# Block-diagonal attention and a gated FFN on one core: first loads in two-token runs, weight signs by a leaky slope, separate first buffers

## The chip, the cores and the metric

The kernel runs on one core of a Trainium2 chip. The core has five engines that work side by side: PE (TensorE, matmuls and the loading of their weights), DVE (VectorE), ACT (ScalarE), POOL (GpSimd), and SP (SyncE), which here issues all DMAs on one queue that 16 DMA engines serve. The metric is the device time of one execution in microseconds (us); the median of 3 runs before is 494.02 us.

## The reference

Attention inside chunks of 64 tokens, for 8 batches, 8 heads, 576 tokens and head size 64, and then an FFN with a gate made by a convolution over 3 neighbouring tokens:

```python
scores = scale * np.matmul(q_c, k_c.transpose(0, 1, 2, 4, 3))     # chunks of 64 tokens
attn = np.exp(scores - np.max(scores, axis=-1, keepdims=True))
attn = attn / (np.sum(attn, axis=-1, keepdims=True) + 1e-09)
x = np.matmul(attn, v_c)                       # then to [8, 576, 512]
h = np.maximum(x @ w_in, 0.0)                  # 512 -> 1024
conv_out[s] = sum(conv_w[k] * h[s + k - 1] for k in range(3))     # zeros beyond the ends
out = (h * sigmoid(conv_out)) @ w_out          # 1024 -> 512
```

q, k and v arrive as float32. [...]

## The kernel before, in words

**Tiles.** 4608 tokens make 36 tiles of 128 (two chunks of 64, not always of one batch). The FFN works on 16 units of 288 tokens: the first matmul of the FFN (`mm1`, L334) runs over a unit with 2 neighbours, in 8 blocks f of 128 hidden columns; the second (`mm2`, L388) over tiles of 128 tokens. Both are made of three products of high and low parts (`x_h`, `x_l`, `wi_h`, `wi_l` and so on), to reach f32 precision with rounded inputs. An `mm1` block is 12 matmuls, an `mm2` step 3.

**A tile of attention.** `load_rows` (L113) loads q and k of tiles 0 to 8 by rows, tokens in partitions, so that a run in memory is one token of one head, 64 numbers. Later tiles come through `load_group` in another layout and are transposed by DVE. `load_v` loads v in four DMAs of 64 partitions. For tiles 0 to 8 `t_pe` (L164) transposes q and then k on PE, four matmuls each into a PSUM bank; `t_copy` (L168, ACT) copies them out. Then come `scores` (L200: 16 matmuls of 64x64), maximum and subtraction (L210, L214, DVE), exp (L223, ACT), sum and reciprocal (L230 to L236, DVE), division (L262, POOL), transpose of the probabilities (`p_pe`, L269, PE), copy (L274, ACT), attention times v (`attn_v`, L283, PE), and the split into `x_h` (L319, ACT) and `x_l` (L323, DVE). The first unit of the FFN needs tiles 0 to 2.

**Weights.** `split` turns a piece of weights into high and low parts. `w_load` (L408) brings it into one of two places (`w_slots`) as low and high words L and H. `w_scale` (L421, ACT) scales H, read as an f32; `w_shift` (L425, DVE) shifts the exponent into place, which throws the sign out; `w_words` (L430, DVE) puts in the upper bits of L; `w_sgn` (L435, DVE) puts back the sign from H, after which the place is free; `w_hi` (L471, ACT) rounds to the high part, and `w_left` (L439, POOL) subtracts for the low part. This happens ten times in 8 MB of weights; conv_w takes another path.

**Places.** Two places for rows (`slots`) and two for weights (`w_slots`) are cut out of the same two tiles of the pool `raw` (L106 to L108), which later hold the groups of q and k.

**The order.** All work is entered as steps with an engine, a cost, and what each needs and frees. A list of step numbers, `order_`, gives the order of all steps, and so of the instructions on each engine and of SP's DMAs. Costs and lags of the steps give each a begin and an end. Where that plan leaves PE idle in the first 110 us, it puts transposes of the identity (L907), one for each 0.14 us, into a free bank; nobody reads their result:

```python
            for _ in range(int((begin[i] - pe_free) / 0.14) if idle else 0):
                nc.tensor.transpose(out=banks[idle[-1]][:, 0:P], in_=ident, identity=ident)
```

They are instructions like others: once built in, they run, whether PE has something to wait for or not.

Of the kernel before, what the change touches and what calls it, by code (L numbers as in the profile page):

```python
# [30 lines left out]
def attn_ffn(ctx: ExitStack, tc: tile.TileContext, q, k, v, w_in, conv_w, w_out, out):  # L31
    nc = tc.nc
# [24 lines left out]
    TP = 12  # L57
    scale = 1.0 / float(D) ** 0.5

    const = ctx.enter_context(tc.tile_pool(name="const", bufs=1))  # L60
    raw = ctx.enter_context(tc.tile_pool(name="raw", bufs=2))
# [5 lines left out]
    work7 = ctx.enter_context(tc.tile_pool(name="work7", bufs=7))  # L67
    ps_s = ctx.enter_context(tc.tile_pool(name="ps_s", bufs=1, space=PSUM))
# [37 lines left out]
    spare = [raw.tile([P, 2 * G * 4 * TG * 32], F32, name="qk") for _ in range(2)]  # L106
    slots = [sp[:, 2048:3072] for sp in spare]
    w_slots = [sp[:, 0:2048] for sp in spare]  # L108
# [14 lines left out]
    def load_group(j):  # L123

        groups[j] = r = raw.tile([P, 2, G, 4 * TG, 32], F32, name="qk")
# [17 lines left out]
    def load_v(st, t):  # L143
# [8 lines left out]
        for s in range(2):  # L152
            b, t0 = chunk(2 * t + s)
            for hp in range(2):
                j0 = 64 * (hp ^ s)
                nc.sync.dma_start(out=r[j0:j0 + C, :, s, :], in_=v[b, hp::2, t0:t0 + C, :].rearrange("g j d -> j g d"))  # L156


    def t_pe(st, i):

        tp = banks[st["tp", i]]
        rows = row_slot(st)[:, 512 * i:512 * i + 512]
        for g in range(G):
            nc.tensor.transpose(out=tp[:, P * g:P * g + P], in_=rows[:, P * g:P * g + P], identity=ident)  # L164

    def t_copy(st, i):
        st[i] = tT = work.tile([P, G, 2 * C], F32, name="qk"[i] + "T")
        nc.scalar.copy(out=tT, in_=banks[st["tp", i]].rearrange("p (g i) -> p g i", i=P))  # L168
# [107 lines left out]
    def attn_v(st):  # L276
        for g in range(G):
            for s in range(2):
                for hp in range(2):
                    j0, n, m = C * (hp ^ s), s, s  # L280
# [137 lines left out]
    def w_scale(st):  # L418

        st["T"] = w_tile(st, "wt")  # L420
        nc.scalar.mul(out=st["T"], in_=st["H"].bitcast(F32), mul=2.0 ** -112)  # L421
# [10 lines left out]

    def w_sgn(st):
        T = st["T"].bitcast(U32)
        nc.vector.scalar_tensor_tensor(out=T, in0=st["H"], scalar=0x80000000, in1=T,  # L435
                                       op0=ALU.bitwise_and, op1=ALU.bitwise_or)
# [62 lines left out]
    def split(key, t_load, src, hi=None, lo=None, lo_pool=False, half=False):  # L499
# [19 lines left out]
        s3 = step("DVE", b, key + 0.01, w_words, (st,), [s2], port=True)  # L519
        s4 = step("DVE", b, key + 0.02, w_sgn, (st,), [s3], free=["wslot"], port=True)  # L520
# [8 lines left out]
    def att(t, key, load_key, writes):  # L529

        st = {"t": t}
        if t < NAT:
            r = "wslot" if t in W_ROWS else "slot"
            ld = step("SP", 1.2 if (2 * t) % NCK < NCK - 1 else 2.3, load_key, load_rows, (st, t), take=[(r, st)], lag=3.3)
            tt = []
            for i in range(2):
                s = step("PE", 0.44, key - 3, t_pe, (st, i), [ld, before.get("t")], take=[("bk", st, ("tp", i)), "qk"[i] + "T"], free=[r] if i else [])
                before["t"] = s
                tt.append(step("ACT", 0.59, key - 3, t_copy, (st, i), [s], free=[("bk", ("tp", i))]))
# [7 lines left out]
        ldv = step("SP", 2.2 if t < TP else 0.5 if (2 * t) % NCK < NCK - 1 else 1.0, load_key + 0.05 if t < 5 else key - 8, load_v, (st, t), [before.get("v")], take=["v"], lag=1.66)  # L547
# [137 lines left out]
    for u in range(NU + 1):  # L685
# [267 lines left out]
```

## Time and profile before

| | before |
|---|---|
| median of 3 runs | 494.02 us (493.81 to 494.75) |
| profiled execution | 494.31 us, span 492.4 us |
| PE, DVE, ACT, POOL busy | 485.1, 350.4, 298.8, 191.6 us |
| granted TensorE clock | 1.000 |
| DMA | 50.16 MB in 185905 packets, of which 175068 under 512 B |
| filler L907 on PE | 160 transposes |
| first `mm1` matmul (L334) starts | 35.91 us |

The span runs from the first to the last instruction of the profiled execution; some 1.9 us of its time lie around it. Busy time on PE counts the filler too. A wait on a row of the profile is idle time of an engine, put down to what ended last before it went on.

### The profile page before, as it was taken

What the parts mean: (1) busy time and instruction counts of PE and PEld (TensorE: products, weight loads), DVE (VectorE), ACT (ScalarE), POOL (GpSimd) and SP (SyncE); (2) the same over time, 40 slices, a digit from 0 to 9 for tenths busy, and PEclk for the clock granted to TensorE, in tenths of its full rate; (3) what the DMA queues carried; (4) which work ended last, traced back from release to release, by engine and by line L of the source; (5) the groups of instructions that cost most, each with busy time, mean ns of one, the idle gap of its engine ahead of it and who ended that gap; (6) DMA issues with size and microseconds to landing.
All of it is one profiled execution on the core that took longest, in us unless ns stands there. A gap on an engine that the chain in (4) does not pass through costs nothing.

```text
span 492.4 us, 12912 instructions
## 1 busy us (share of the span) xinstructions
PE 485.1 (99%) x4985; PEld 436.2 (89%) x4985; DVE 350.4 (71%) x736; ACT 298.8 (61%) x749; POOL 191.6 (39%) x261
## 2 busy tenths in 40 slices
PE   8999999999999999999999999999999999999997
PEld 8889989999888998989888999899988988999885
DVE  3889998687566778886857887888878685574300
ACT  4479988875634675765635767566665564775501
POOL 1253538433314161534543173415253515244300
PEclk9999999999999999999999999999999999999999
DMA  8998964423255664436555553236561111100102
GB/s 196 232 233 240 236 166 79 71 46 57 64 124 114 134 156 73 96 68 137 89 116 133 119 87 75 62 70 137 103 166 46 44 44 44 47 19 2 43 23 85
DMA packets 185905, 50.16 MB, mean 102 GB/s; under 512 B 175068, under 2 KB 178164, under 8 KB 185844
## 3 DMA queue, kind: packets, MB, share of 16 engines
q1 hardware_dynamic: 185844, 49.34, 44.6%
q8 instruction: 39, 0.64, 0.6%
q14 instruction: 22, 0.18, 0.1%
HBM read 36.72 MB, written 9.44 MB: 94 GB/s over the span
## 4 chain that ended last, share of the span: by engine, by line
PE 93%; DMA 2%; DVE 2%; ACT 1%; SPq 1%; issue 0%; ACTq 0%
PE b_ps L388 41%; PE b_ps L334 41%; PE sx_ps L200 3%; PE sx_ps L283 2%; DMA qk<-in_moe_w_in 2%; PE z_ps L283 1%; PE b_ps L164 1%; PE z_ps L200 1%; PE b_ps L269 1%; PE b_ps L907 1%; DVE wt L430 1%; SPq L156 0%; DVE wt L435 0%; ACT wt L421 0%; ACT wi_h L471 0%
## 5 line engine op out<-in xcount | busy, mean ns | idle before, releaser
L379 POOL TENSOR_TENSOR g_l<-c,g_h 128x288 fp32r<-128x288 f32 (+8 forms) x184 | 109.9, 620 | 162.2 <-ACT g_h L375 132.0
L388 PE MATMUL b_ps<-wo_h,g_h 128*128 128x512 f32 x288 | 115.6, 401 | 0.0
L388 PE MATMUL b_ps<-wo_h,g_l 128*128 128x512 f32 x288 | 113.6, 395 | 0.0
L388 PE MATMUL b_ps<-wo_l,g_h 128*128 128x512 f32 x288 | 113.4, 394 | 0.0
L350 DVE SCALAR_TENSOR_TENSOR c<-b_ps,cw,c 128x287 f32<-128x287 f32 (+1 forms) x128 | 65.2, 512 | 46.0 <-ACT c L346 45.8
L334 PE MATMUL b_ps<-x_h,wi_h 128*128 128x290 f32 x512 | 90.6, 299 | 0.0
L334 PE MATMUL b_ps<-x_l,wi_h 128*128 128x290 f32 x512 | 89.5, 297 | 0.0
L334 PE MATMUL b_ps<-x_h,wi_l 128*128 128x290 f32 x512 | 89.1, 296 | 0.0
L334 PEld LDWEIGHTS b_ps<-x_h,wi_h 128*128 128x128 f32 x512 | 79.3, 189 | 7.5 <-DVE c L365 0.2
L341 ACT ACTIVATE b_ps<-b_ps 128x290 f32<-128x290 f32 x128 | 50.9, 399 | 53.3 <-PE b_ps L334 52.6
L362 ACT ACTIVATE c<-c 128x288 f32<-128x288 f32 x128 | 56.4, 443 | 43.6 <-DVE c L356 43.1
L365 DVE SCALAR_TENSOR_TENSOR c<-c,b_ps 128x288 f32<-128x288 f32 x128 | 56.7, 447 | 28.6 <-ACT c L362 27.9
L334 PEld LDWEIGHTS b_ps<-x_l,wi_h 128*128 128x128 f32 x512 | 75.9, 190 | 0.0
L334 PEld LDWEIGHTS b_ps<-x_h,wi_l 128*128 128x128 f32 x512 | 75.4, 189 | 0.0
L346 ACT ACTIVATE c<-b_ps,cw 128x288 f32<-128x288 f32 x128 | 63.4, 500 | 7.0
L356 DVE SCALAR_TENSOR_TENSOR c<-b_ps,cw,c 128x288 f32<-128x288 f32 (+1 forms) x128 | 64.9, 511 | 2.8
L388 PEld LDWEIGHTS b_ps<-wo_h,g_l 128*128 128x128 f32 x288 | 54.2, 188 | 12.6
L375 ACT CAST g_h<-c 128x288 fp32r<-128x288 f32 (+8 forms) x184 | 58.7, 357 | 9.2 <-DVE c L365 7.2
L388 PEld LDWEIGHTS b_ps<-wo_h,g_h 128*128 128x128 f32 x288 | 54.4, 189 | 9.3
L388 PEld LDWEIGHTS b_ps<-wo_l,g_h 128*128 128x128 f32 x288 | 54.3, 188 | 8.3
L245 POOL TENSOR_TENSOR wt<-wt,z 128x512 f32<-128x512 f32 x24 | 25.1, 1051 | 63.5 <-DVE z L233 14.3
L393 ACT ACTIVATE wt<-b_ps 128x512 f32<-128x512 f32 x36 | 21.4, 598 | 35.7 <-PE b_ps L388 27.4
(64 smaller groups left out, 495.1 us busy)
## 6 DMA issues: line engine op xcount, KB each, us to landing
out<-wt SPq DMA_DIRECT2D x36, 256.0 KB, 2.4
v<-in_v SPq DMA_DIRECT2D x21, 256.0 KB, 3.4
qk<-in_q SPq DMA_DIRECT2D x96, 48.0 KB, 2.3
qk<-in_k SPq DMA_DIRECT2D x96, 48.0 KB, 2.3
qk<-in_moe_w_out SPq DMA_DIRECT2D x4, 1024.0 KB, 6.5
v<-in_v SPq DMA_DIRECT2D x48, 64.0 KB, 3.6
wt<-wt SPq DMA_DIRECT2D x48, 64.0 KB, 2.1
qk<-in_q SPq DMA_DIRECT2D x96, 24.0 KB, 1.9
```

Of the source, the lines that this page charges most:

```text
L245: nc.gpsimd.tensor_tensor(out=two(st, "to"), in0=two(st, "of"), in1=z, op=ALU.mult)
L334: nc.tensor.matmul(h_ps[:, 0:hi - lo], lhsT=wt[:, f // 2, kt, P * (f % 2):P * (f % 2) + P], rhs=xt[:, u % NX, kt, 0:hi - lo], start=n == 0 ...
L341: nc.scalar.activation(out=h, in_=h, func=AF.Relu)
L346: nc.scalar.mul(out=st["c"], in_=banks[st["h"]][:, i0:i0 + st["n"]], mul=cw[:, FT + f:FT + f + 1])
L350: nc.vector.scalar_tensor_tensor(out=c[:, a:n], in0=banks[st["h"]][:, i0 + a - 1:i0 + n - 1], scalar=cw[:, f:f + 1], in1=c[:, a:n], op0=AL ...
L356: nc.vector.scalar_tensor_tensor(out=c[:, 0:b], in0=banks[st["h"]][:, i0 + 1:i0 + 1 + b], scalar=cw[:, 2 * FT + f:2 * FT + f + 1], in1=c[: ...
L362: nc.scalar.activation(out=st["c"], in_=st["c"], func=AF.Tanh, scale=0.5)
L365: nc.vector.scalar_tensor_tensor(out=st["c"], in0=st["c"], scalar=1.0, in1=banks[st["h"]][:, st["i0"]:st["i0"] + st["n"]], op0=ALU.add, op ...
L375: nc.scalar.copy(out=g_h[:, f, gs], in_=st["c"][:, cs])
L379: nc.gpsimd.tensor_tensor(out=g_l[:, f, gs], in0=st["c"][:, cs], in1=g_h[:, f, gs].bitcast(F32), op=ALU.subtract)
L388: nc.tensor.matmul(banks[st["o"]], lhsT=gt[:, f, o:o + P], rhs=wt[:, f, :], start=f == 0 and n == 0, stop=f == FT - 1 and n == 2)
L393: nc.scalar.mul(out=st["os"], in_=banks[st["o"]], mul=0.5)
```

## The change

- q and k of tiles 0 to 4 (`NP = 5`): a partition takes two neighbouring tokens instead of one, so that a run in memory is 128 numbers. q goes into the even partitions, k into the odd ones. `t_pe` picks them out with every other column of the identity (`ident[:, i::2]`), in 16 matmuls that contract over 128 partitions and have 64 columns on each side, in place of 4 transposes; `t_copy` puts even and odd tokens back in turn.
- The sign of the weights: `w_scale` is an activation with a leaky slope. A negative number is multiplied by another 2^32, which sets the bit that the shift moves into the sign's place. `w_sgn` goes, and `w_words` frees the place.
- Places for rows and weights are four tiles of a pool of their own, closed when the first group is loaded.
- v of tiles 0 to 11 in 3 DMAs where both chunks are of one batch (4 before, and 4 still where they aren't); which of the two chunks a half of `v` holds changes with it.
- The costs in the plan follow (`t_pe` 0.9 for 0.44, lags of the loads), and `order_` is another list: the order of most steps is new.

```diff
+    NP = 5
...
-    spare = [raw.tile([P, 2 * G * 4 * TG * 32], F32, name="qk") for _ in range(2)]
-    slots = [sp[:, 2048:3072] for sp in spare]
-    w_slots = [sp[:, 0:2048] for sp in spare]
+    places = sb_w.enter_context(tc.tile_pool(name="first", bufs=1))
+    slots = [places.tile([P, 2 * DM], F32, name=f"qk{i}") for i in range(2)]
+    w_slots = [places.tile([P, 4 * DM], F32, name=f"w{i}") for i in range(2)]
...
     def load_rows(st, t):
+        if t < NP:
+            r = row_slot(st).rearrange("(p two) (h c) -> two p h c", two=2, h=H)
...
+                    nc.sync.dma_start(out=r[i, p0:p0 + n], in_=src[b, :, t_:t_ + 2 * n, :].rearrange("h (p e) d -> p h (e d)", e=2))
...
     def load_group(j):
-        groups[j] = r = raw.tile([P, 2, G, 4 * TG, 32], F32, name="qk")
+        if not groups:
+            sb_w.close()
+            groups["raw"] = ctx.enter_context(tc.tile_pool(name="raw", bufs=2))
+        groups[j] = groups["raw"].tile([P, 2, G, 4 * TG, 32], F32, name="qk")
...
-        for s in range(2):
-            b, t0 = chunk(2 * t + s)
-            for hp in range(2):
-                j0 = 64 * (hp ^ s)
-                nc.sync.dma_start(out=r[j0:j0 + C, :, s, :], in_=v[b, hp::2, t0:t0 + C, :].rearrange("g j d -> j g d"))
+        (b0, t0), (b1, t1) = chunk(2 * t), chunk(2 * t + 1)
+        for hp in range(2):
+            for b, t_, j0, n in [(b0, t0, 0, P)] if b0 == b1 and not hp else [(b0, t0, C * hp, C), (b1, t1, C - C * hp, C)]:
+                nc.sync.dma_start(out=r[j0:j0 + n, :, hp, :], in_=v[b, hp::2, t_:t_ + n, :].rearrange("g j d -> j g d"))
...
+        if st["t"] < NP:
+            r = row_slot(st).rearrange("p (g u e d) -> p g u e d", g=G, u=2, e=2)
+            for g in range(G):
+                for e in range(2):
+                    for u in range(2):
+                        nc.tensor.matmul(tp.rearrange("p (g e n) -> p g e n", g=G, e=2)[D * u:D * u + D, g, e],
+                                         lhsT=r[:, g, u, e], rhs=ident[:, i::2], start=True, stop=True)
+            return
...
-        nc.scalar.mul(out=st["T"], in_=st["H"].bitcast(F32), mul=2.0 ** -112)
+        nc.scalar.activation(out=st["T"], in_=st["H"].bitcast(F32), func=AF.Prelu, scale=2.0 ** -112, alpha=2.0 ** 32)
...
-    def w_sgn(st):
-        T = st["T"].bitcast(U32)
-        nc.vector.scalar_tensor_tensor(out=T, in0=st["H"], scalar=0x80000000, in1=T,
-                                       op0=ALU.bitwise_and, op1=ALU.bitwise_or)
...
-        s3 = step("DVE", b, key + 0.01, w_words, (st,), [s2], port=True)
-        s4 = step("DVE", b, key + 0.02, w_sgn, (st,), [s3], free=["wslot"], port=True)
+        s4 = step("DVE", b, key + 0.01, w_words, (st,), [s2], free=["wslot"], port=True)
```

**How the order moves.** The lines of the functions move down: L164 becomes L177 for tiles 0 to 4 (L182 for 5 to 8), L200 L221, L269 L290, L283 L304, L334 L355, L907 L921; `qk_103` and `qk_104` are the two places for rows, `w_105` and `w_106` those for weights.

PE at the start of the program, before (`x50` is the number of matmuls in a row):

```order
L907 MATMUL b_ps<-ident 128x128 x50
L164 MATMUL b_ps<-ident,qk 128x128 x4
L907 MATMUL b_ps<-ident 128x128
L164 MATMUL b_ps<-ident,qk 128x128 x4
L907 MATMUL b_ps<-ident 128x128 x6
L200 MATMUL sx_ps<-kT,qT 64x64 x16
```

and after:

```order
L921 MATMUL b_ps<-ident 128x128 x42
L177 MATMUL b_ps<-ident,qk_103 64x64 x16
L921 MATMUL b_ps<-ident 128x128
L177 MATMUL b_ps<-ident,qk_103 64x64 x16
L921 MATMUL b_ps<-ident 128x128
L177 MATMUL b_ps<-ident,qk_104 64x64 x16
L921 MATMUL b_ps<-ident 128x128
L177 MATMUL b_ps<-ident,qk_104 64x64 x16
L221 MATMUL sx_ps<-kT,qT 64x64 x16
```

Eight fillers fewer stand ahead of the first transposes, and both tiles' transposes now stand ahead of the first scores.

PE from the second attention step to the first FFN matmul, before:

```order
L283 MATMUL sx_ps<-pT,v 64x64 x16
L907 MATMUL b_ps<-ident 128x128 x2
L164 MATMUL b_ps<-ident,qk 128x128 x4
L907 MATMUL b_ps<-ident 128x128 x2
L164 MATMUL b_ps<-ident,qk 128x128 x4
L907 MATMUL b_ps<-ident 128x128 x6
L200 MATMUL sx_ps<-kT,qT 64x64 x16
L907 MATMUL b_ps<-ident 128x128 x3
L283 MATMUL sx_ps<-pT,v 64x64 x16
L269 MATMUL b_ps<-ident,e 128x128 x4
L907 MATMUL b_ps<-ident 128x128 x10
L334 MATMUL b_ps<-x_h,wi_h 128x290 x4
```

and after:

```order
L304 MATMUL sx_ps<-pT,v 64x64 x16
L921 MATMUL b_ps<-ident 128x128 x4
L290 MATMUL b_ps<-ident,e 128x128 x4
L177 MATMUL b_ps<-ident,qk_103 64x64 x16
L921 MATMUL b_ps<-ident 128x128 x2
L221 MATMUL sx_ps<-kT,qT 64x64 x16
L921 MATMUL b_ps<-ident 128x128 x2
L304 MATMUL sx_ps<-pT,v 64x64 x16
L177 MATMUL b_ps<-ident,qk_103 64x64 x16
L921 MATMUL b_ps<-ident 128x128 x7
L355 MATMUL b_ps<-x_h,wi_h 128x290 x4
```

The scores of tile 4 and the fourth transpose of probabilities have moved behind the first FFN matmul. In the whole program there are 91 fillers (160 before).

SP's queue up to the v of tile 1, before:

```order
L119 DMA qk<-in_q 128x8x64
L119 DMA qk<-in_k 128x8x64
L156 DMA v<-in_v 64x4x64 x4
L119 DMA qk<-in_q 128x8x64
L119 DMA qk<-in_k 128x8x64
L408 DMA qk<-in_moe_w_in 128x2x512
L156 DMA v<-in_v 64x4x64 x4
```

and after:

```order
L120 DMA qk_103<-in_q 64x8x128
L120 DMA qk_103<-in_k 64x8x128
L166 DMA v<-in_v 128x4x64
L166 DMA v<-in_v 64x4x64 x2
L120 DMA qk_104<-in_q 64x8x128
L120 DMA qk_104<-in_k 64x8x128
L429 DMA w_105<-in_moe_w_in 128x2x512
L166 DMA v<-in_v 128x4x64
L166 DMA v<-in_v 64x4x64 x2
```

The loads stand in the same order; the shapes of the runs and the number of v's DMAs are what is new.

More of the change, by code (lines that the diff above doesn't have):

```diff
@@ L57, in attn_ffn @@
     TP = 12
+    NP = 5
     scale = 1.0 / float(D) ** 0.5
     const = ctx.enter_context(tc.tile_pool(name="const", bufs=1))
-    raw = ctx.enter_context(tc.tile_pool(name="raw", bufs=2))
     rawv = ctx.enter_context(tc.tile_pool(name="rawv", bufs=4))
@@ L67, in attn_ffn @@
     work7 = ctx.enter_context(tc.tile_pool(name="work7", bufs=7))
+    sb_w = ExitStack()
     ps_s = ctx.enter_context(tc.tile_pool(name="ps_s", bufs=1, space=PSUM))
@@ L113, in load_rows @@
     def load_rows(st, t):
+        if t < NP:
+            r = row_slot(st).rearrange("(p two) (h c) -> two p h c", two=2, h=H)
+            (b0, t0), (b1, t1) = chunk(2 * t), chunk(2 * t + 1)
+            for i, src in enumerate((q, k)):
+                for b, t_, p0, n in [(b0, t0, 0, C)] if b0 == b1 else [(b0, t0, 0, C // 2), (b1, t1, C // 2, C // 2)]:
+                    nc.sync.dma_start(out=r[i, p0:p0 + n], in_=src[b, :, t_:t_ + 2 * n, :].rearrange("h (p e) d -> p h (e d)", e=2))
+            return
         r = row_slot(st).rearrange("p (i c) -> p i c", i=2)
@@ L151, in load_v @@
             return
-        for s in range(2):
-            b, t0 = chunk(2 * t + s)
-            for hp in range(2):
-                j0 = 64 * (hp ^ s)
-                nc.sync.dma_start(out=r[j0:j0 + C, :, s, :], in_=v[b, hp::2, t0:t0 + C, :].rearrange("g j d -> j g d"))
+        (b0, t0), (b1, t1) = chunk(2 * t), chunk(2 * t + 1)
+        for hp in range(2):
+            for b, t_, j0, n in [(b0, t0, 0, P)] if b0 == b1 and not hp else [(b0, t0, C * hp, C), (b1, t1, C - C * hp, C)]:
+                nc.sync.dma_start(out=r[j0:j0 + n, :, hp, :], in_=v[b, hp::2, t_:t_ + n, :].rearrange("g j d -> j g d"))
     def t_pe(st, i):
         tp = banks[st["tp", i]]
+        if st["t"] < NP:
[5 more added lines that the diff above has]
+                                         lhsT=r[:, g, u, e], rhs=ident[:, i::2], start=True, stop=True)
+            return
         rows = row_slot(st)[:, 512 * i:512 * i + 512]
@@ L167, in t_copy @@
         st[i] = tT = work.tile([P, G, 2 * C], F32, name="qk"[i] + "T")
+        if st["t"] < NP:
+            nc.scalar.copy(out=tT.rearrange("p g (n e) -> p g e n", e=2), in_=banks[st["tp", i]].rearrange("p (g e n) -> p g e n", g=G, e=2))
+            return
         nc.scalar.copy(out=tT, in_=banks[st["tp", i]].rearrange("p (g i) -> p g i", i=P))
@@ L279, in attn_v @@
                 for hp in range(2):
-                    j0, n, m = C * (hp ^ s), s, s
+                    j0, n, m = C * (hp ^ s), hp, s
                     if st["t"] >= TP:
@@ L533, in att @@
             r = "wslot" if t in W_ROWS else "slot"
-            ld = step("SP", 1.2 if (2 * t) % NCK < NCK - 1 else 2.3, load_key, load_rows, (st, t), take=[(r, st)], lag=3.3)
+            ld = step("SP", 1.2 if (2 * t) % NCK < NCK - 1 else 2.3, load_key, load_rows, (st, t), take=[(r, st)], lag=2.2 if t < NP else 3.1)
             tt = []
             for i in range(2):
-                s = step("PE", 0.44, key - 3, t_pe, (st, i), [ld, before.get("t")], take=[("bk", st, ("tp", i)), "qk"[i] + "T"], free=[r] if i else [])
+                s = step("PE", 0.9 if t < NP else 0.44, key - 3, t_pe, (st, i), [ld, before.get("t")], take=[("bk", st, ("tp", i)), "qk"[i] + "T"], free=[r] if i else [])
                 before["t"] = s
-                tt.append(step("ACT", 0.59, key - 3, t_copy, (st, i), [s], free=[("bk", ("tp", i))]))
+                tt.append(step("ACT", 0.63 if t < NP else 0.59, key - 3, t_copy, (st, i), [s], free=[("bk", ("tp", i))]))
             slot_users.append(s)
@@ L546, in att @@
                 tt[1]["free"] = ["grp"]
-        ldv = step("SP", 2.2 if t < TP else 0.5 if (2 * t) % NCK < NCK - 1 else 1.0, load_key + 0.05 if t < 5 else key - 8, load_v, (st, t), [before.get("v")], take=["v"], lag=1.66)
+        ldv = step("SP", (1.7 if (2 * t) % NCK < NCK - 1 else 2.2) if t < TP else 0.5 if (2 * t) % NCK < NCK - 1 else 1.0, load_key + 0.05 if t < 5 else key - 8, load_v, (st, t), [before.get("v")], take=["v"], lag=1.55)
         tt[0]["after"] += [before["T"]] if t else []
```

243 rows, old and new, of the table order_ are left out of this document.

## The prediction

> **What bounds the kernel now.** I read the page's engine line first, then TensorE's (PE's) waits over the whole span and over the span from 44 us on, then its timeline up to the first matmul of the FFN.
>
> ```profile
> PE 485.1 (99%) x4985; PEld 436.2 (89%) x4985; DVE 350.4 (71%) x736; ACT 298.8 (61%) x749; POOL 191.6 (39%) x261
> ...
> PE b_ps L907 <- POOL ident masks.py:199: 1.4, 1, 1.4
> PE sx_ps L200 <- ACT kT L168: 0.9, 2, 0.6
> PE b_ps L486 <- DVE wt L483: 0.7, 1, 0.7
> PE sx_ps L283 <- issue: 0.4, 2, 0.3
> PE b_ps L269 <- POOL e L262: 0.2, 1, 0.2
> ...
> PE sx_ps L200 <- ACT kT L168: 0.3, 1, 0.3
> ```
>
> PE is busy for 99% of the span, and its waits add up to 3.6 us. The last row is the only wait left in the window from 44 us to the end: 0.3 us in 448. So from there on PE alone sets the time, and nothing that shortens DVE, ACT or a transfer after 44 us counts. But busy isn't useful:
>
> ```profile
> L907 PE MATMUL b_ps<-ident 128*128 128x128 f32 x160 | 23.6, 293 | 1.4 <-POOL ident masks.py:199 1.4
> ...
> 1.36 7.69 PE L907 MATMUL b_ps<-ident 128*128 128x128 f32 x50 [1.36 <-POOL ident masks.py:199]
> 8.89 0.60 PE L164 MATMUL b_ps<-ident,qk 128*128 128x128 f32 x4
> 9.33 0.27 PE L907 MATMUL b_ps<-ident 128*128 128x128 f32 x1
> ...
> 11.34 0.69 PE L200 MATMUL sx_ps<-kT,qT 64*64 64x64 f32 x32 [0.65 <-ACT kT L168]
> 11.96 0.87 PE L907 MATMUL b_ps<-ident 128*128 128x128 f32 x6
> ...
> 18.61 0.24 PE L486 MATMUL b_ps<-ident,wt 24*128 24x24 f32 x1 [0.65 <-DVE wt L483]
> ...
> 25.41 0.60 PE L269 MATMUL b_ps<-ident,e 128*128 128x128 f32 x4
> 25.84 0.71 PE L907 MATMUL b_ps<-ident 128*128 128x128 f32 x5
> ...
> 33.78 0.69 PE L283 MATMUL sx_ps<-pT,v 64*64 64x64 f32 x32
> 34.41 0.66 PE L269 MATMUL b_ps<-ident,e 128*128 128x128 f32 x4
> 34.91 1.25 PE L907 MATMUL b_ps<-ident 128*128 128x128 f32 x10
> 35.91 0.79 PE L334 MATMUL b_ps<-x_h,wi_h 128*128 128x290 f32 x4
> ```
>
> L907 multiplies the identity by itself: filler, put where the plan sees PE idle, with a result that nobody reads. All but two stand before 35.91 us, when the first FFN matmul (L334) starts. The time therefore moves by what this opening gains or loses in filler and waits, plus what is added to PE's useful work.
>
> **The opening as a sum, before.** From start to start, a transpose step of q or k (L164) takes 9.33 - 8.89 = 0.44 us, a score step 11.96 - 11.34 = 0.62, a transpose of probabilities (L269) 0.43 to 0.50, say 0.46, attention times v (L283) 34.41 - 33.78 = 0.63, the one of conv_w 0.2. Between 8.89 and 35.91 stand 10, 5, 4, 3 and 1 of these: 4.4 + 3.1 + 1.84 + 1.89 + 0.2 = 11.4 us. The other 15.6 of the 27.0 us are 108 fillers and the waits near them, 0.145 us for each filler.
>
> **The transposes in pieces.** For tiles 0 to 4, 10 steps of 4 transposes become 10 steps of 16 matmuls over 128 rows and 64 columns. The trace has no such matmul. The nearest rows are the scores: 16 matmuls of 64 by 64, each two instructions in the trace, and four such squares fit the array.
>
> ```profile
> 188.99 0.93 PE sx_ps L200 x64
> ```
>
> Two tiles of scores take 0.93 us in a stretch without filler, 0.465 each; standing alone a score step took 0.62, so 0.155 is the change of shape. A piece over all rows fills half the array instead of a quarter: twice 0.465 is 0.93, and I take 1.0 us, between 0.93 and 0.93 + 0.155. Below, 0.62, if it ran like a score step. Above: L164's transposes are 0.11 us each, half as many columns 0.055, and 32 of them in single file 1.75, with the change of shape 1.9.
>
> A rule speaks against this part. The Trainium skill, "TensorE: Matmul & The Clock Gate", section "The mechanism", says that a weight load overlaps running matmuls only where their row group differs, and all 16 pieces have the same rows. By the figures of that page (64 columns at 1.2 per ns to load, at 2.4 to stream) 32 pieces in single file would be an estimated 2.6 us a step, 16 us more in the whole than I count. L164 above disagrees: its transposes also use all rows, and four start within 0.44 us although each matmul row lasts 0.27.
>
> **The opening after.** In the new program's order 42 fillers stand ahead of the first transpose step (50 before). The last of the 50 are 0.11 us apart, so it starts at 8.89 - 0.95 = 7.95 us. From there to the first L334 (now L355) are 10 steps in pieces, 4 scores, 3 transposes of probabilities, 3 attention steps, the one of conv_w, and 48 fillers: 10.0 + 2.48 + 1.38 + 1.89 + 0.2 + 48 x 0.145 (6.95) = 22.9. The FFN begins at 30.85, 5.06 us earlier. One score step and one transpose of probabilities are now behind that point: 0.62 + 0.46 = 1.08 back. Net -4.0 us.
>
> **Whether the data come in time.** The fillers only say what the plan expects. What ends last before 35.91 is attention of tile 2, at 33.78; in the new order it starts at 28.2 (the same sum without 7 fillers, a step in pieces and itself). So tile 2's v must land 5.6 us sooner. The next rows are stretches of 2 us (engines, granted clock, DMA share, GB/s) and SP's issues.
>
> ```profile
> 8.00:10.00 2.00, 2.00 (x21) 2.00 (x20) 1.59 (x3) 0.83 (x2) 0.00 (x0) 1.00 1.31 218
> 10.00:12.00 2.00, 1.35 (x40) 1.05 (x38) 0.00 (x0) 1.29 (x3) 1.27 (x1) 1.00 0.64 120
> 12.00:14.00 2.00, 2.00 (x23) 2.00 (x20) 1.90 (x6) 0.92 (x3) 0.00 (x0) 1.00 1.02 399
> 16.00:18.00 2.00, 1.96 (x18) 1.72 (x16) 1.93 (x6) 0.80 (x2) 0.00 (x0) 1.00 0.62 105
> ...
> 9.72 0.39 SPq L408 DMA_DIRECT2D qk<-in_moe_w_in  x1
> 20.56 2.59 SPq L156 DMA_DIRECT2D v<-in_v  x4
> 27.20 2.58 SPq L156 DMA_DIRECT2D v<-in_v  x4
> ```
>
> At 8 to 10 us only q and k move, in runs of 256 B: 218 GB/s. At 12 to 14 it is mostly w_in, in runs of 2 KB: 399. Per engine of 16 that is 18.8 ns for 256 B and 82 ns for 2 KB, a line with 0.0353 ns per byte; 512 B come out at 27.8 ns, 295 GB/s, an estimate from these two rows. The q and k of a tile (524 KB) then take 1.78 us and not 2.40: 0.62 saved, with 0 (no faster) and 1.09 (as fast as w_in) as ends. Five tiles lie ahead of tile 2's v: 3.1 us. Its own four issues take 2.58 us, 0.65 each; three make 1.94, and three tiles 1.9 us. That is 5.0 of the 5.6. The rest should come from the idle DMA of 10 to 12 and 16 to 18 us: w_in's third load is issued at 9.72 only because a place for weights is held until then.
>
> ```profile
> 8.24 0.69 DVE L430 SCALAR_TENSOR_TENSOR wt<-qk,wt 128x512 uint32<-128x512 uint32 x1
> 8.97 0.69 DVE L435 SCALAR_TENSOR_TENSOR wt<-qk,wt 128x512 uint32<-128x512 uint32 x1
> ...
> L435 DVE SCALAR_TENSOR_TENSOR wt<-qk,wt 128x1024 uint32<-128x1024 uint32 x6 | 7.3, 1216 | 0.1
> L435 DVE SCALAR_TENSOR_TENSOR wt<-qk,wt 128x512 uint32<-128x512 uint32 x4 | 2.8, 692 | 0.1
> L168 ACT COPY kT<-b_ps 128x512 f32<-128x512 f32 x9 | 5.3, 590 | 3.3 <-PE b_ps L164 3.2
> L89 ACT ACT_TABLE_LOAD x1 | 1.3, 1283 | 0.7 <-PEq L938 0.7
> ```
>
> **The sign by the slope.** The step at L435 goes: 6 x 1.216 + 4 x 0.692 = 10.1 us of DVE. It ends at 9.66 and the load is issued at 9.72, so each place is free 0.7 to 1.2 us sooner; that is the missing 0.6 and some to spare. The rest lies beside PE. On ACT the same activation runs with another function. I cost it at nothing: the new order holds one table load, as before. If each of the 10 needed its own table and one back, that would be 20 x 1.283 = 26 us of ACT, an end I give no weight. The 10 copies that now write every other column I leave at 0.59 us; if one took twice as long, ACT would have 5.9 us more before 40 us, about half a copy in the way of each tile. Own buffers cost and save nothing by themselves; PE has no wait on the group loads behind them (first wait list).
>
> **The sum.** 494.31 us is the profiled execution, 492.4 of it the span and 1.9 around it. 494.3 - 4.0 = 490.3; the median of the runs, 494.02, is 0.3 lower, so I forecast 490.0. With 0.93 for a step in pieces it is 489.3, with 1.085 it is 490.9. The likeliest case's own range is 488.8 to 491.6.
>
> **Rivals.** Within 0.2% (1.0 us) a measurement of this kernel can hardly tell a change from none.
>
> 1. The pieces run in single file (1.9 us a step). Then the FFN begins 9 us later than I count, the net is +5.0, and the time 499. It turns from gain to loss at 1.4 us a step. For it: no row has pieces over 128 rows and 64 columns, and fillers can't give way, since they are instructions. Against it: four quarter-array matmuls do run side by side (0.465 us for 32). 0.08; the skill's rule above, which would make it 506, is in this share.
>
> 2. Runs of 512 B are no faster, so the wider loads don't do what they are for. Then only the v issues (1.9 us) help: attention of tile 2 at 31.9, the FFN at 31.9 + 0.63 + 1.0 + 0.9 = 34.4, 1.5 sooner less 1.08: net -0.4, 493.6. Against it: 399 against 218 GB/s for longer runs. 0.11.
>
> 3. The opening gets shorter, but ACT then holds PE back.
>
> ```profile
> 40.00:50.00 10.00, 9.72 (x129) 9.16 (x128) 9.58 (x19) 9.20 (x21) 3.40 (x2) 1.00 0.89 233
> 50.00:60.00 10.00, 10.00 (x130) 9.53 (x130) 10.00 (x20) 9.88 (x22) 5.30 (x5) 1.00 0.91 231
> 60.00:70.00 10.00, 10.00 (x119) 8.65 (x118) 9.95 (x23) 9.07 (x21) 5.24 (x5) 1.00 0.85 204
> ```
>
> DVE and ACT (third and fourth number of busy time) are at 9.1 to 10.0 of 10 us there, with the weights still being converted. DVE loses 10 us of work, ACT none. If ACT's work can't move forward, PE can gain no more than ACT's idle time in these 30 us, 0.80 + 0.12 + 0.93 = 1.85, for 492.2. Against it: ACT's conversions start when loads land, and those come sooner too. 0.12.
>
> 4. The pieces run as cheaply as scores (0.62) and data come early: up to 3.8 more, of which waits in the opening take about half: 488.1. 0.06.
>
> **Chances.** My case 0.63, rivals 0.08, 0.11, 0.12 and 0.06. Faster takes my case, the third and fourth and a little of the second: 0.82; same the rest of the second: 0.09; slower the first and a remainder: 0.09. The range, 488.2 to 493.4, leaves out the first, half of the second and the tails.
>
> **What would show it.** Right: first transpose step near 8.0 us; a step in pieces 0.9 to 1.1 from start to start; first L355 at 30 to 32; over 270 GB/s where only q and k move; no PE wait over 0.5 us behind that point. A step over 1.4, waits of PE on v ("issue" ahead of L304), or PE waits on ACT between 35 and 65 us would prove me wrong.

## The result, and the profile after

| | before | after |
|---|---|---|
| median | 494.12 us (493.73 to 494.75, 20 executions) | 498.38 us (493.55 to 505.72, 20 executions) |
| profiled execution | 494.31 us, span 492.4 | 495.24 us, span 493.1 |
| fillers on PE | 160 | 91 |
| first FFN matmul | 35.91 us | 33.01 us |

The change makes the kernel slower: the ratio of times is 1.006 [1.0037, 1.0083], and 1.0045 [1.0027, 1.0063] in 12 more executions (median 496.74). The ratios leave disturbed executions out and so lie below the quotient of the medians. The forecast was 490.0 us.

The page's engine line, after:

```profile
PE 484.8 (98%) x5196; PEld 433.8 (88%) x5196; DVE 342.0 (69%) x726; ACT 299.4 (61%) x749; POOL 190.9 (39%) x261
```

PE's waits over the whole span (total, times, longest):

```profile
PE b_ps L355 <- DVE c L386: 2.3, 2, 2.1
PE b_ps L921 <- POOL ident masks.py:199: 1.4, 1, 1.4
PE b_ps L177 <- DMA qk<-in_k: 0.6, 1, 0.6
PE sx_ps L221 <- DVE e L235: 0.3, 1, 0.3
```

Before, the longest wait behind 44 us was 0.3 us. Now a matmul of the FFN waits 2.1 us for DVE's `c` (L386, which frees a PSUM bank). The opening on PE's timeline:

```profile
1.36 6.66 PE L921 MATMUL b_ps<-ident 128*128 128x128 f32 x42 [1.36 <-POOL ident masks.py:199]
8.57 1.15 PE L177 MATMUL b_ps<-ident,qk 128*64 128x64 f32 x32 [0.55 <-DMA qk<-in_k]
9.65 0.33 PE L921 MATMUL b_ps<-ident 128*128 128x128 f32 x1
9.91 1.16 PE L177 MATMUL b_ps<-ident,qk 128*64 128x64 f32 x32
11.00 0.33 PE L921 MATMUL b_ps<-ident 128*128 128x128 f32 x1
...
32.27 0.98 PE L921 MATMUL b_ps<-ident 128*128 128x128 f32 x7
33.01 0.78 PE L355 MATMUL b_ps<-x_h,wi_h 128*128 128x290 f32 x4
```

A step in pieces takes 9.65 - 8.57 = 1.08 us (1.09 the next), the first waits for k until 8.57, and the FFN starts 2.90 us sooner than before. The long wait, read on PE, DVE, POOL and SP in turn (the timelines of each engine):

```profile
174.92 0.40 PE L409 MATMUL b_ps<-wo_h,g_l 128*128 128x512 f32 x1
177.38 0.80 PE L355 MATMUL b_ps<-x_h,wi_h 128*128 128x290 f32 x4 [2.06 <-DVE c L386]
...
180.17 1.11 PE L221 MATMUL sx_ps<-kT,qT 64*64 64x64 f32 x64
...
171.96 0.52 DVE L377 SCALAR_TENSOR_TENSOR c<-b_ps,cw,c 128x287 f32<-128x287 f32 x1
175.69 1.30 DVE L280 STREAM_TRANSPOSE pT<-wt 128x512 f32<-128x512 f32 x2 [3.21 <-DMA wt<-wt]
176.91 0.41 DVE L386 SCALAR_TENSOR_TENSOR c<-c,b_ps 128x288 f32<-128x288 f32 x1
...
167.06 1.05 POOL L270 TENSOR_TENSOR wt<-wt,z 128x512 f32<-128x512 f32 x1
...
168.60 2.23 SPq L150 DMA_DIRECT2D qk<-in_q  x4
170.93 0.41 SPq L417 DMA_DIRECT2D out<-wt  x1
171.45 2.60 SPq L276 DMA_DIRECT2D wt<-wt  x4
```

From the bottom up: POOL has divided the probabilities by 168.1, but SP issues the four DMAs that swap their blocks (L276) only from 171.45 to 174.05, behind group loads and a store. DVE's copy of them (`pT`, L280) waits 3.21 us for these, and `c` (L386) stands behind the copy in DVE's queue though it doesn't need it. PE stands.

### The profile page after: what moved, and what is told of

It reads as the page before. It is cut to its first block, busy times and chain, and to the rows that moved or that the text cites. A ratio compares the mean times of both kernels' runs of the same rounds, so it can differ in the third digit from the quotient of the medians.

```text
span 493.1 us, 13309 instructions
## 1 busy us (share of the span) xinstructions
PE 484.8 (98%) x5196; PEld 433.8 (88%) x5196; DVE 342.0 (69%) x726; ACT 299.4 (61%) x749; POOL 190.9 (39%) x261
## 4 chain that ended last, share of the span: by engine, by line
PE 91%; DVE 3%; DMA 2%; POOL 1%; SPq 1%; ACT 1%; issue 1%; DVEq 0%; POOLq 0%
PE b_ps L355 40%; PE b_ps L409 38%; PE sx_ps L304 3%; PE sx_ps L221 3%; PE b_ps L177 2%; PE z_ps L304 1%; DMA qk<-in_k 1%; PE b_ps L921 1%; PE z_ps L221 1%; PE b_ps L290 1%; POOL g_l L400 1%; DMA wt<-wt 1%; PE b_ps L182 1%; SPq L276 1%; DVE e L235 0%
## 5 line engine op out<-in xcount | busy, mean ns | idle before, releaser
L371 DVE SCALAR_TENSOR_TENSOR c<-b_ps,cw,c 128x287 f32<-128x287 f32 (+1 forms) x128 | 64.4, 508 | 72.5 <-ACT c L367 72.1
L355 PE MATMUL b_ps<-x_h,wi_h 128*128 128x290 f32 x512 | 90.8, 299 | 2.3 <-DVE c L386 2.3
L355 PEld LDWEIGHTS b_ps<-x_h,wi_h 128*128 128x128 f32 x512 | 79.8, 189 | 12.7 <-DVE c L386 3.9
L355 PE MATMUL b_ps<-x_l,wi_h 128*128 128x290 f32 x512 | 89.5, 297 | 0.0
L355 PE MATMUL b_ps<-x_h,wi_l 128*128 128x290 f32 x512 | 89.2, 296 | 0.0
L386 DVE SCALAR_TENSOR_TENSOR c<-c,b_ps 128x288 f32<-128x288 f32 x128 | 56.7, 445 | 32.8 <-ACT c L383 32.4
L355 PEld LDWEIGHTS b_ps<-x_l,wi_h 128*128 128x128 f32 x512 | 75.7, 189 | 0.0
L355 PEld LDWEIGHTS b_ps<-x_h,wi_l 128*128 128x128 f32 x512 | 75.4, 189 | 0.0
L377 DVE SCALAR_TENSOR_TENSOR c<-b_ps,cw,c 128x287 f32<-128x287 f32 (+1 forms) x128 | 65.1, 511 | 2.8
L414 ACT ACTIVATE wt<-b_ps 128x512 f32<-128x512 f32 x36 | 21.4, 596 | 18.2 <-PE b_ps L409 18.0
```

The source lines that it names most:

```text
L355: nc.tensor.matmul(h_ps[:, 0:hi - lo], lhsT=wt[:, f // 2, kt, P * (f % 2):P * (f % 2) + P], rhs=xt[:, u % NX, kt, 0:hi - lo], start=n == 0 ...
L371: nc.vector.scalar_tensor_tensor(out=c[:, a:n], in0=banks[st["h"]][:, i0 + a - 1:i0 + n - 1], scalar=cw[:, f:f + 1], in1=c[:, a:n], op0=AL ...
L377: nc.vector.scalar_tensor_tensor(out=c[:, 0:b], in0=banks[st["h"]][:, i0 + 1:i0 + 1 + b], scalar=cw[:, 2 * FT + f:2 * FT + f + 1], in1=c[: ...
L386: nc.vector.scalar_tensor_tensor(out=st["c"], in0=st["c"], scalar=1.0, in1=banks[st["h"]][:, st["i0"]:st["i0"] + st["n"]], op0=ALU.add, op ...
L414: nc.scalar.mul(out=st["os"], in_=banks[st["o"]], mul=0.5)
```

## The experiments

The changed kernel is taken apart in four ways: by the stretch of its order, by its parts, by SP's queue, and at last by the one wait. Times in brackets are the lowest and highest of the executions. For kernels with mixed orders the edit is the list `order_` alone: it takes the steps that one plan begins before a border, and then the remaining steps in the order of the other.

**A second look.** The changed kernel once more, profiled (`again`).

> The changed kernel once more, for a second profile. Both theories: first FFN matmul near 33.0 us again, and a time anywhere from 493.5 to 503. Theory A (the new order behind the opening leaves too little slack, and a chain through SP, POOL and DVE stops PE): whatever the time is above 492 shows as PE waits behind 120 us. Theory B (one of the new parts disturbs PE, for instance its clock): the loss shows as slower matmuls at a lower granted clock without waits ahead of them.

495.35 us, span 493.4, first FFN matmul at 33.45, the wait on `c` 0.9 us at 175 and one on ACT's copy `wt` (L414) of 0.6 at 285. The wait on `c` is there again, with another size. The second one marks another tight place of the new order: the kernels `old_open_new_late`, `few_fillers`, `four_transposes` and `rows_copies_later` below have it too, between 287 and 295 us, with 1.0 to 1.3 us.

**Which half of the order.** `parts_old_order`: all parts of the change, before's order to the end. `new_open_old_late`: the new order to 62 us, before's behind. `old_open_new_late`: before's to 56 us, the new one behind.

> All new parts (loads of two tokens, pieces, slope, own places, v in 3 loads), but the list of step numbers is that of the kernel before, without the removed sign steps. Theory A: the spread goes; all runs within 1 us of each other and 494 to 497 (10 pieces steps cost 6.5 us more PE, fewer fillers pay for part of it). Theory B: runs spread over several us as those of the changed kernel, median 497 or more.

> The changed kernel with its own order for what its plan begins before 62 us, and the order of the kernel before for all later steps. Theory A: the opening's gain of about 1.8 us stays and nothing is lost later: 492 to 493, spread under 1 us. Theory B: spread and median as in the changed kernel, 496 to 500.

> The changed kernel's parts with the order of the kernel before up to 56 us, and the changed kernel's order for all later steps. Theory A: spread over several us stays, median 498 to 502, with PE waits behind 120 us. Theory B: the same spread, so this run tells little under it; a tight 494 to 496 would speak against A.

| | old later order | new later order |
|---|---|---|
| old opening | 497.47 (497.29 to 497.92), 1.0058 [1.0042, 1.0074] | 504.18 (502.16 to 505.46), 1.0183 [1.0154, 1.0211] |
| new opening | 494.23 (493.28 to 495.21), 0.9992 [0.9977, 1.0007] | 498.38, 1.006 [1.0037, 1.0083] |

The new later order costs 4.2 us behind the new opening and 6.7 behind the old one; the new opening gains 3.2 and 5.8. The cell of the changed kernel is its first 20 executions, taken apart from the other three. By the ratios the later order costs 0.68% (3.4 us) and 1.25% (6.2 us); with the ratio of the changed kernel's 12 later executions, 1.0045, the first is 0.53% (2.6 us). PE's waits in the kernel with the old opening and the new later order:

```profile
PE b_ps L355 <- DVE c L386: 3.3, 2, 1.7
PE sx_ps L221 <- ACT qT L189: 1.7, 1, 1.7
...
PE b_ps L409 <- ACT wt L414: 1.0, 1, 1.0
```

The two on `c` end at 63.6 and 185.0 us, the others at 67.2 and 294.6. The two kernels of the table with the old later order have no wait over 0.5 us behind the opening. So the later order brings the waits, not a part of the change; where they stand depends on the opening ahead of it.

**Which part.** `slope_only`: before, with the leaky slope alone. `rows_old_order`: before's order with slope, own places and v in 3 loads, q and k by rows (the edit against the changed kernel below, with before's order). `rows_new_open_old_late`: the same edit with the new order to 62 us.

```diff
-    NP = 5
+    NP = 0
```

> The kernel before with its own order, and of the whole change only the slope: the sign step issues nothing. DVE loses 10 us. If the slope alone made the 0.9 us that slope, places and v loads gained together: 492.8 to 493.4. If the v loads did it, since data of tile 2's v end the opening: 493.8 to 494.3.

> Order of the kernel before, with the slope, the own places and v in 3 loads, but q and k of tiles 0 to 4 loaded and transposed as before (256-byte runs, 4 transposes). If the pieces alone cost the 3.3 us of the run with all parts in the old order: 493.6 to 494.6, as before. If slope, places or v loads cost something: above 495. If they gain: below 493.

> New order up to 62 us, order of the kernel before behind it, slope, own places, v in 3 loads, but q and k of tiles 0 to 4 in rows as before (256-byte runs, 4 transposes, 159 fillers). If two-token runs pay for their pieces: the FFN begins later than 33.0, and the time is above 494.2. If they don't: it begins at 31 to 33, 492 to 493.5.

`slope_only` 493.49 us (492.84 to 494.67), ratio 0.9989 [0.998, 0.9999]; `rows_old_order` 493.08 (492.40 to 493.67), 0.9973 [0.9957, 0.9988], with the FFN from 35.11; `rows_new_open_old_late` 494.03 (493.47 to 496.18), 1.0006 [0.9995, 1.0017], from 33.31. Under before's order the slope pays 0.1%, and slope, own places and three v loads together 0.3%. Pieces and two-token loads cost 497.47 - 493.08 = 4.4 us under before's order, where the FFN starts at 39.40 with them, and 0.2 (nothing that can be told) in the new opening with before's later order. The plan counts less for a step by rows and so puts in more fillers (150 against 132 in the first pair, 159 against 94 in the second); the pairs differ in this too. `rows_old_order` is faster than both kernels.

`four_transposes` leaves the changed kernel's plan, order and fillers and takes the pieces away; the even and odd tokens of q and k then come out mixed, so it is there for its time alone:

```diff
-        if st["t"] < NP:
-            r = row_slot(st).rearrange("p (g u e d) -> p g u e d", g=G, u=2, e=2)
...
-            return
```

> The changed kernel, plan and order and the 91 fillers untouched, but each of the 10 steps in pieces issues the 4 plain transposes on the same loaded rows (tokens of q and k come out mixed, so the output isn't the reference's). A step is 0.44 and not 1.09 us, so the opening can meet the plan that the order was made for. Theory S (the late order loses because the opening is late against its plan): the FFN begins at 29.5 to 31, no wait of PE over 0.5 us behind 120 us, 488.5 to 491, spread under 2 us. Theory L (the late order itself is too tight): the FFN begins that early too, but PE still waits for DVE near 175 us, and runs spread over 491 to 498.

494.67 us (492.38 to 497.82), 1.0003 [0.9977, 1.0029]. PE's timeline at the start:

```profile
9.15 0.63 PE L174 MATMUL b_ps<-ident,qk 128*128 128x128 f32 x4 [0.76 <-DMA qk<-in_k]
9.62 0.27 PE L913 MATMUL b_ps<-ident 128*128 128x128 f32 x1
...
10.64 0.63 PE L174 MATMUL b_ps<-ident,qk 128*128 128x128 f32 x4 [0.21 <-DMA qk<-in_k]
```

A step takes 0.47 us in place of 1.08, 6.1 us less for ten, but the FFN starts at 31.31, 1.7 sooner: PE waits for k instead (0.76 and 0.21) and for the divided probabilities (1.8). The profiled execution (497.12 us, span 495.1) gives this back later: PE waits 1.9 us on `c` up to 176.3, with a granted clock of 0.66 and then 0.50 in the two stretches of 2 us from 176, and 1.3 us on ACT up to 287.1. A still shorter opening doesn't make the later order run without waits.

**Fillers.** `few_fillers` keeps only the 42 fillers ahead of the first transposes; `few_fillers_old_late` does so with before's order behind 62 us.

```diff
-            for _ in range(int((begin[i] - pe_free) / 0.14) if idle else 0):
+            for _ in range(int((begin[i] - pe_free) / 0.14) if idle and pe_free == 2.0 else 0):
```

> The changed kernel with the 42 fillers ahead of the first transposes and none of the 49 later ones. Theory S (the opening runs some 3 us behind the order's plan because a step in pieces is 1.09 us and not 0.9; SP, whose queue is full and in order, carries the delay on, and swaps and loads of q and k come late at 140 to 180 us): the FFN begins at 30 to 31.5 and not 33.0, and the loss behind 120 us goes: 490 to 492, spread under 2 us. Theory L (the late order is too tight however early the opening ends): the FFN begins earlier too, but runs still spread over 494 to 500 with PE waits at 170 to 190 us.

> The new opening with the late order of the kernel before, and only the first 42 fillers. Both theories: FFN at 30 to 31.5 instead of 33.0, nothing lost later, so 1.5 to 3 us under the same kernel with fillers (494.2): 491 to 492.7. If fillers only stand where PE would wait for data anyway, the FFN still begins near 33 and the time stays at 494.

498.78 us (497.24 to 503.21), 1.0109 [1.0078, 1.0139], and 494.53 (491.61 to 497.02 but for one of 940.47), 1.000 [0.9978, 1.0022]. The first one's stretches from 16 us (PE, PEld, DVE, ACT, POOL, granted clock, DMA share, GB/s):

```profile
16.00:20.00 4.00, 3.12 (x65) 3.03 (x65) 3.48 (x10) 1.15 (x2) 1.04 (x1) 0.71 0.79 211
20.00:24.00 4.00, 4.00 (x105) 3.35 (x105) 2.53 (x4) 1.26 (x3) 1.04 (x1) 0.87 0.84 226
...
28.00:32.00 4.00, 3.90 (x92) 3.45 (x96) 2.41 (x4) 2.90 (x6) 2.58 (x3) 0.59 0.84 261
```

The granted clock falls to 0.59 in the opening, where it was 1.00 with fillers, and the FFN still starts at 33.32, and at 32.11 in the second kernel, where 30 to 31.5 was expected. Leaving fillers out thus saves nothing in the changed kernel; what they cost by themselves isn't separated, since steps now run at the lower clock. The later order's loss (498.78 against 494.53) stays without them.

**SP's queue.** `stores_on_act` issues the 36 output stores from ACT, `swaps_on_pool` the swaps from POOL.

```diff
-        nc.sync.dma_start(out=out_rows[P * t:P * t + P, :], in_=st["os"])
+        nc.scalar.dma_start(out=out_rows[P * t:P * t + P, :], in_=st["os"])
...
-            nc.sync.dma_start(out=to[o:o + 32, :, 1 - a % 2], in_=of[i:i + 32, :, a % 2])
+            nc.gpsimd.dma_start(out=to[o:o + 32, :, 1 - a % 2], in_=of[i:i + 32, :, a % 2])
```

> The changed kernel with the 36 stores of the output issued by ACT right behind the copies that they wait for, not by SP. Theory S: SP is no longer held by stores, its loads and swaps come 3 to 5 us sooner at 140 to 175 us, and PE's wait near 175 us goes: 492 to 494, spread under 2 us. Theory L with another cause than SP (POOL or DVE too late): no change, 494 to 502.

> The changed kernel with the swaps of probabilities (4 DMAs for a pair of tiles, which wait for POOL) issued on POOL's queue behind the multiplication that they wait for, so that SP's loads of q and k never stand behind them. Theory Q (SP's queue, held by swaps that wait for POOL, is what passes a delay on from pair to pair): PE's wait near 175 us goes, 492 to 494, spread under 2 us. If POOL's or DVE's own place in the order decides: no better than 494 to 502.

The first takes 506.68 us (503.70 to 511.78), 1.0254 [1.0216, 1.0292]. Its PE waits:

```profile
PE b_ps L355 <- ACT wt L414: 5.2, 2, 3.6
PE b_ps L355 <- DVE c L386: 3.7, 2, 3.0
```

Two of its stretches (columns as above):

```profile
306.00:308.00 2.00, 0.00 (x0) 0.00 (x0) 0.00 (x0) 0.00 (x0) 0.00 (x0) 1.00 0.32 51
...
310.00:312.00 2.00, 2.00 (x9) 1.71 (x9) 1.64 (x6) 0.86 (x3) 0.18 (x1) 0.58 0.36 68
```

Without the stores SP issues the swap for the copy at 175 us earlier:

```profile
170.12 2.60 SPq L276 DMA_DIRECT2D wt<-wt  x4
```

This is 1.33 us ahead of the changed kernel, and PE's wait there is gone. Others take its place: 0.7 us up to 171.9, and longer ones that end at 258, 309 and 364 us; behind the longest the granted clock is 0.58. The second takes 496.23 (495.29 to 501.19), 1.0056 [1.0032, 1.0079], with 1.33 us on `c` at 175 and 1.46 on ACT at 413. POOL has issued the swap by 171.29, 2.76 us sooner than SP did, but DVE's copy starts only 0.51 us sooner (175.18). So SP's queue carries a part of the delay at this place, and in neither run does relieving it make the kernel faster.

**A series of borders.** The new order to 110, 200 and 350 us of the plan, before's behind, and the changed kernel, all on one chip.

> The changed kernel with its new order for the steps that the plan begins before 110 us, and the order of before for the rest. Known: the same with the border at 62 us takes 494.2 us, and the new order to the end 498.4. If the loss is made between 62 and 110 us, this takes 496 or more; if the chain of swap, copy and PE near 175 us makes it, 494.0 to 494.8, and no PE wait over 1 us at 170 to 180 us.

> As before, with the border at 200 us of the plan. If the loss is made by the one chain near 175 us (PE idle for 2.06 us there), this takes 495.5 to 496.5 and has that wait; if it is spread over the whole later order, about a third of the 4.2 us, 495.5, without one such place; if it is made behind 200 us, 494.0 to 494.8.

> As before, with the border at 350 us of the plan. If the loss is made at 175 us, this takes what the border at 200 us takes (within 0.5 us); if it is spread over the whole, 497; if it is made at the very end, 494.0 to 494.8.

> The changed kernel itself, on the same chip and in the same rounds as the three others: the end of the series of borders. 498.4 us if the median of its first runs holds; if these were spread by the chip, less, down to 495.3 (its two profiled executions).

| border | median | ratio | span of the profile | waits on `c` there |
|---|---|---|---|---|
| 110 us | 496.17 (495.36 to 500.39) | 1.0044 [1.0026, 1.0062] | 493.8 | 1.5 at 119.7 |
| 200 us | 499.27 (496.63 to 501.33) | 1.0104 [1.0072, 1.0135] | 494.9 | 2.3 near 177 |
| 350 us | 495.31 (493.84 to 499.41) | 1.0023 [1.0002, 1.0045] | 492.0 | 0.9 near 177 |
| none | 496.74 (494.67 to 500.05) | 1.0045 [1.0027, 1.0063] | 494.6 | 2.0 near 177 |

The times don't rise with the border, so a loss spread evenly over the later order is out; but the border at 110 us makes a wait of its own, the one at 200 us takes more than was expected of a loss made at 175 us (495.5 to 496.5), and the one at 350 us takes 4.0 us less than that at 200, where the same was expected. The series doesn't name the place. In its profiled executions the span goes with the size of the one wait; `again`, with 0.9 us and a span of 493.4, shows that this wait isn't all. In the changed kernel's execution here the clock answers to it:

```profile
174.00:176.00 2.00, 1.42 (x9) 0.94 (x7) 0.30 (x1) 0.90 (x2) 0.00 (x0) 1.00 0.44 107
176.00:178.00 2.00, 0.61 (x3) 0.61 (x4) 2.00 (x5) 0.00 (x0) 0.00 (x0) 0.92 1.02 188
178.00:180.00 2.00, 2.00 (x11) 2.00 (x9) 1.04 (x3) 0.00 (x0) 0.00 (x0) 0.50 0.30 47
180.00:182.00 2.00, 2.00 (x90) 1.72 (x93) 0.50 (x1) 1.43 (x5) 0.00 (x0) 0.73 0.33 52
```

and PE's timeline there:

```profile
177.39 1.11 PE L355 MATMUL b_ps<-x_h,wi_h 128*128 128x290 f32 x4 [1.97 <-DVE c L386]
...
181.67 0.52 PE L221 MATMUL sx_ps<-kT,qT 64*64 64x64 f32 x24
```

After 1.97 us of waiting the granted clock is 0.50 and then 0.73 (the number ahead of the last two), and the next four matmuls take 1.11 us in place of 0.80. From the end of the wait to the scores of the group it is 181.67 - 177.39 = 4.28 us here and 180.17 - 177.38 = 2.79 in the first profile, where the clock stayed at 1.00: 1.5 us more, behind a wait that was no longer.

**The one wait.** `copies_later` is the changed kernel with two steps of the list moved. DVE's queue, against the changed kernel's:

```diff
 L377 SCALAR_TENSOR_TENSOR c<-b_ps,cw,c 128x287
+L386 SCALAR_TENSOR_TENSOR c<-c,b_ps 128x288
+L371 SCALAR_TENSOR_TENSOR c<-b_ps,cw,c 128x288
 L280 STREAM_TRANSPOSE pT<-wt 128x2x8x32 x2
-L386 SCALAR_TENSOR_TENSOR c<-c,b_ps 128x288
-L371 SCALAR_TENSOR_TENSOR c<-b_ps,cw,c 128x288 x2
+L371 SCALAR_TENSOR_TENSOR c<-b_ps,cw,c 128x288
```

`rows_copies_later` is the same with `NP = 0`.

> The changed kernel with one move of its order: on VectorE the two copies of pT near 175 us stand behind the next c (L386) and the next L371, no longer ahead of them; nothing else changes. If the copies that wait for the swap are what holds PE, and this costs about 2 us and at times more by a lower granted clock behind it, then no PE wait over 0.5 us stands at 170 to 180 us, the span is 490.8 to 491.8 and the median 493 to 495, with a smaller spread. If the later order is late in many places, the wait comes back within the next 60 us and the median stays at 496 to 498.

> The same move, and q and k of tiles 0 to 4 by rows as before (four transposes, runs of 256 B), under the new order. If the pieces and the two-token loads pay nothing in the new opening, this takes what the other kernel of this call takes, within 0.5 us; if they pay, 1 us or more above it.

494.55 us (492.49 to 502.58), 1.0004 [0.9979, 1.0028], and 496.19 (494.32 to 499.67), 1.0039 [1.0022, 1.0055]. The only wait of PE from 34 us to the end in `copies_later`:

```profile
PE sx_ps L304 <- DVE pT L280: 0.3, 1, 0.3
```

and DVE's and PE's timelines at the place:

```profile
173.33 0.45 DVE L386 SCALAR_TENSOR_TENSOR c<-c,b_ps 128x288 f32<-128x288 f32 x1 [0.51 <-ACT c L383]
176.06 1.30 DVE L280 STREAM_TRANSPOSE pT<-wt 128x512 f32<-128x512 f32 x2 [1.32 <-DMA wt<-wt]
...
175.49 0.69 PE L355 MATMUL b_ps<-x_h,wi_h 128*128 128x290 f32 x4
177.17 1.42 PE L304 MATMUL z_ps<-pT,v 64*64 64x64 f32 x64
```

The swap and the copy are no sooner than in the changed kernel (175.69 there), but `c` no longer stands behind them, and PE works through. No other wait takes the place in this execution: the span is 491.9 us against 493.1 and 494.6. That the executions would also lie closer together did not come; the longest has a granted clock of 0.992, and where it waited isn't recorded. Of the 12 executions 4 take over 496 us; of the changed kernel's 32 timed ones it was 23, of 149 of the kernel before, over all chips, 6 (one of 1214.61 us left out). With the move, loads by rows cost 1.6 us against the pieces, where the earlier pair of kernels showed 0.2; the FFN starts at 36.13 against 33.70, but in the longest of the 12 executions. There PE waits 0.6 us for the moved copy itself (`pT`, up to 180.5).

## Why the prediction was wrong

**The step that failed: "from there on PE alone sets the time, and nothing that shortens DVE, ACT or a transfer after 44 us counts".** The row behind it (one wait of 0.3 us) was read from before's trace, and the change replaced the order of that very stretch. The sum priced the opening and carried the rest over unchanged. In the new order a copy that hangs on POOL, SP and a swap stands ahead of a `c` that PE needs. The 2x2 table puts the price of the new later order at 4.2 us by the medians and 3.4 by the ratios. In the profiled executions, whose spans are 1.8 and 3.3 us over that of `new_open_old_late` (491.3), the one wait is large enough for it: 2.06 us, or 1.97 and some 1.5 of lower clock. The first of them is 3.1 us under the median of its 20 executions, though, and what the longer ones wait for isn't recorded. Moving two steps of the list took it away and brought the ratio from 1.0045 [1.0027, 1.0063] to 1.0004 [0.9979, 1.0028]. The two kernels ran on different chips and the intervals touch, so the size of this gain is less certain than the cause of the wait, which the rows show. The third rival had the manner of it, an opening that gets shorter and another engine that gives it back, but with ACT between 40 and 70 us; it came from DVE at 175, and neither DVE nor ACT was full there.

**Terms of the opening that were mis-sized.** The forecast had the FFN at 30.85; it starts at 33.01, 2.16 later:

- A step in pieces measured 1.085 (mean of the two above), not 1.0: 0.85 us for ten. The upper end of the range given was right, the choice within it wrong. Single file (1.9) is out, and with it the rule of the Trainium skill that was weighed against it ("TensorE: Matmul & The Clock Gate", "The mechanism"): the estimate of 2.6 us a step from that page's figures disagrees with the trace's 1.08.
- The first step starts at 8.57, not 7.95: 0.62. I counted fillers only; 0.55 of it is the wait for k, and 0.07 a slip, since eight fillers 0.11 us apart are 0.88 and not 0.95.
- The rest takes 33.01 - 8.57 - 10.85 = 13.59, not 12.90: 0.69, of it 0.28 in the wait on DVE's `e`; the other 0.41 isn't placed. The v of tile 2 was issued at 23.69 and not 27.20, 3.5 us sooner, where 5.0 were counted.

The opening therefore gains 2.90 us, less 1.08 for the two steps behind it: 1.8 and not 4.0. With the two waits on `c`, 2.3 us, in place of before's 0.3, this gives +0.2 against a measured +0.7 in the span. The measured span is longer than the same sum gives in `copies_later` and `new_open_old_late` too, by 0.7 and 1.0 us, so the 1.08 may be too small as well; that isn't tested.

**What was right.** The runs of 512 B, estimated at 295 GB/s, in the stretches where little but q and k moves (after; last column GB/s; conv_w's 24 KB are issued at 7.22, a load of w_in at 8.59):

```profile
7.00:8.00 1.00, 1.00 (x10) 0.78 (x8) 0.74 (x3) 0.34 (x1) 0.00 (x0) 1.00 1.20 301
8.00:9.00 1.00, 0.45 (x15) 0.46 (x16) 0.52 (x1) 0.45 (x1) 0.00 (x0) 1.00 1.16 280
```

Before, 218 was measured from 8 to 10 us. The slope, which works on the high one of the two 32-bit words of each float64 weight, costs ACT nothing: 967 ns for a piece (mean of ten) before and after, and one table load. The sign step was all but hidden (`slope_only` 0.9989). The v of tile 1 was issued in 1.79 us (1.94 forecast), but those of tiles 0 and 2 took 2.72 and 2.52. Of the signs to look for, a step in pieces of 0.9 to 1.1 us and over 270 GB/s came; the first step near 8.0 failed by 0.57 us, the FFN at 30 to 32 by 1.0, and "no PE wait over 0.5 us behind that point" by 1.6.

**What stays open.** Why the swap comes late relative to PE has more than one cause: SP's queue carries only a part of it. Whether pieces and two-token loads pay at all depends on the order, and on the fillers that come with it (+4.4, +0.2 and -1.6 us in three pairs). And `copies_later` is even with before, not ahead of it by the opening's 1.8 us; its profiled execution had the FFN from 33.70 and a span 0.5 us shorter than before's, and the longer executions have no profile. The tight place near 290 us, on ACT's `wt`, was left as it is in all runs.

## What to carry to other kernels

A stretch without waits is evidence for the order it was measured in; when a change rewrites the order, look on each engine's new queue for an instruction that hangs on a long chain (here POOL, SP, DMA) and has one behind it that the bottleneck engine needs. Such a copy could stand two places later here without a new wait in the profile, though under other loads PE then waited 0.6 us for the copy itself. And price a stall on PE at more than its length: the clock behind it may fall as well, by an estimated 1.7 us at most for each fall here (see below).

## What the runs showed of the hardware

- Idle time on PE of about 2 us lowers the granted clock in some executions and not in others. In the same program 2.06 us left it at 1.00 and 1.97 us brought 0.92, 0.50 and 0.73 in three stretches of 2 us. Waits of 2.31 (`new_to_200`) and 2.14 us (`few_fillers`, at 178) left it at 1.00 too; waits of 1.92 (`four_transposes`, at 176) and 1.8 us (`rows_copies_later`, in the opening) brought 0.66 and 0.50, and 0.60 and 0.54.
- A fall cost the same in the four executions worked out here. The 0.92, 0.50 and 0.73 are 0.16 + 1.00 + 0.54 = 1.70 us of full clock lost; 0.66, 0.50 and 0.99 are again 1.70, 0.60 and 0.54 are 1.72, and the 0.58 and 0.57 behind the 3.6 us of `stores_on_act` 1.70: as much as 3.4 us at half the clock. The Trainium skill, "TensorE: Matmul & The Clock Gate", section "The HAM clock gate (the "warmup" mystery)", has a half-rate state and a free-running window of about 3.4 us, which agrees with the 0.50, with these 3.4 us and with the chance in it; that it takes an idle window of that length disagrees, if idle means no work at all, with the 1.97 us here.
- The clock is only a part of the scatter. Executions of the changed kernel (493.55 to 505.72 in its first 20) with a clock of 1.000 still take 493.55 to 496.86, and the longest, with 0.993 over a span of 503.7, lost 3.5 us to it by estimate. The kernel before isn't free of it: 493.73 to 494.75 in the first 20 executions, up to 498.15 (clock 0.997) in later ones.
- Fillers keep the clock up: without 49 of them it was 0.71, 0.87, 0.99 and 0.59 in four stretches of 4 us from 16 us on, where it was 1.00 with them.
- 16 matmuls over 128 rows and 64 columns with a two-column step in the moving identity take 1.08 us, 34 ns for each of 32 instructions, where four transposes of the same data take 0.47.
